# Chunk 0 of a delta-rule attention: the inverse of 64 rows kept as two blocks of 32, applied one behind the other

## The chip, the cores and the metric

The kernel runs on one core of one Trainium2 chip. Five engines work side by side, each with its own queue of instructions that it takes in order: TensorE (PE in the profile, PEld its weight loads), VectorE (DVE), ScalarE (ACT), GpSimd (POOL) and SyncE (SP), which here only issues DMA transfers. Between engines the order is kept by semaphores. The metric is the device time of one execution in microseconds (us).

## The reference

Part one is attention with a delta rule, for 4 batches, 8 heads, 768 tokens and head size 48; each head has a 48x48 state that goes from token to token. Part two takes its output, 3072 tokens with 384 features, through a layer with SiLU.

```python
k_n = k / (norm(k) + 1e-06)
for t in range(S):
    y[:, :, t] = einsum('bhd,bhde->bhe', q[:, :, t], state)
    v_old = einsum('bhde,bhd->bhe', state, k_n[:, :, t])
    state = state + beta[:, :, t] * einsum('bhd,bhe->bhde', k_n[:, :, t], v[:, :, t] - v_old)
x = y.transpose(0, 2, 1, 3).reshape(3072, 384)
h = x @ w_in                       # 384 x 2048
out = (h * (1 / (1 + exp(-h)))) @ w_out
```

The two weights arrive as 64-bit numbers and are narrowed to 32 bits on the chip; all products are in fp32, which TensorE makes in two passes.

## The kernel before

**Tiles.** The 768 tokens are six chunks of 128, a chunk is two halves of 64 tokens (0 and 1), a half two blocks of T = 32, and a block two corners of Q = 16. The 32 pairs of batch and head are taken as two groups (g = 0, 1) of 16, HH in the code. Within a half the recurrence over tokens is solved at once: with the lower triangle of the key products k k^T, scaled by beta, the new values are z = inverse x (V - what the state already holds). `score` makes the key products (pa, kept in aps[c, g][0]; those with the queries in aps[c, g][1]), `inner` applies the inverse xi to the values vf (pz, copied to zbuf), `update` adds to the states (pu), `keys` subtracts what the state holds (ph, by an addition into vf on DVE), `old` and `new` make the outputs (pyc), and for half 0 of chunk 0, where the state is zero, `first_outputs` makes them from a padded copy of z called slab (py).

**The inverse of chunk 0.** `invert_first` solves all corners of 16 at once by a loop of additions on DVE, and transposes the result twice (`low`, `up`). Corners become the inverse of 32 by `corner` (key products times `low`, scaled and completed by DVE into y), `turned` (its transpose, into xes) and `straight` (into xi). Blocks of 32 become the inverse of 64 by two `merge_half` products each. These steps, for both groups, are `joins(hf)`: half 0's run straight through, half 1's are stepped by the words j of the script. All their products are 32 rows by 32 columns, so that four lie side by side in TensorE's array.

**The layer.** A half-chunk's outputs are copied from pyc into xT (features by tokens): the odd heads go through the tile `part` and five DMA transfers by SP, the even heads straight by ACT (`even_heads`, `move`). `hidden(c, hf)` makes phid = w_in^T xT in eight pieces of 2 x 6 passes, ACT applies SiLU to gT, `project` makes po. hidden(0,0) needs half 0's outputs, hidden(0,1) half 1's.

**Narrowing.** The weights come in eight pieces each of w_in ("in", 0 to 7) and w_out ("out", 0 to 7). A piece's raw bits are loaded by SP, and then `narrow` runs two steps on ACT (L232, L233), two on DVE (L237, L241) and one on POOL (L245). f of hidden(0,0) needs piece f.

**What sets the order.** `pin` keeps each engine's instructions in program order. `in_line` does the same for SP's DMA queue and lets each transfer wait for the landing of the one two before it. So the program's order decides, and in the middle of the kernel it is written out by hand as a string of words: s is the next step of `solve`, r the next piece of hidden or project, f and b the next step or beginning of a narrowing, j steps of joins(1), T and q transposes of chunk 1's keys and queries, l its lengths, p its scores, i its inverse, w and W loads of weights. A PSUM bank (`bank`) is one of eight, taken in turn; a product into a bank waits for what last read it. From chunk 1 on nothing is changed; `merge` there does the merges.

Of the kernel before, what the change touches and what calls it, by code (L numbers as in the profile page):

```python
# [19 lines left out]
def kernel(  # L20
# [10 lines left out]
    nc = tc.nc  # L31
# [242 lines left out]
    AT_UP = AT_X + SLAB  # L274
# [63 lines left out]
    second = const.tile([P, 1], FP32, name="second")  # L338
    pin(nc.vector.tensor_reduce(out=second[:], in_=pick[:, T // 2 : T], axis=AX.X, op=ALU.add))
# [324 lines left out]
    def invert_first(step):  # L664
# [7 lines left out]
        for m in range(Q - 1, 0, -1):  # L672
# [16 lines left out]
        y = sum_room[:, AT_G : AT_G + BH * T].rearrange("p (n s) -> p n s", s=T)  # L689
        up = sum_room[:, AT_UP : AT_UP + BH * T].rearrange("p (n t) -> p n t", t=T)  # L690
        pin(nc.vector.transpose(out=low.rearrange("p n s -> p s n"), in_=x[:, 0:Q, :]))
        pin(nc.gpsimd.tensor_copy(
            out=y[:, :, Q:T], in_=pick[:, Q:T].unsqueeze(1).to_broadcast([P, BH, Q])
        ))
# [3 lines left out]
        both = work.tile([P, BH, T], FP32, name="xe_y", tag="g", bufs=1)  # L698
        xes[0], ys[0] = both[:], both[:].rearrange("p (g h) t -> p g h t", g=2)

        def heads(g, hf):
            for i in range(HH // 2):
                for e in range(2):
                    yield i, HH * g + 2 * i + e, hf ^ e ^ g

        def of_half(t, g, hf, k):
            return t[:, HH * g + (hf ^ k ^ g) : HH * (g + 1) : 2]

        def out_of(pl, to, width):
            return pl[to, 0 : HH // 2 * width].rearrange("p (n s) -> p n s", s=width)  # L710

        def corner(g, hf):

            pls = [bank(room, "pl") for room in (A, CC)]
            for i, n, k in heads(g, hf):
                for j in (2 * k, 2 * k + 1):
                    cols = slice(T * (j % 2), T * (j % 2 + 1))
                    pin(nc.tensor.matmul(
                        pls[k][rows[j], Q * i : Q * (i + 1)], lhsT=aps[0, g][0][rows[j], n % HH // H, n % H, cols],
                        rhs=low[rows[j], n, :], start=True, stop=True,  # L720
                    ))
                    yield
            for k in range(2):
                of = slice(W * k, W * (k + 1))
                pin(nc.vector.scalar_tensor_tensor(
                    out=of_half(y[of], g, hf, k)[:, :, 0:Q], in0=out_of(pls[k], of, Q), scalar=second[of],
                    in1=pick[of, 0:Q].unsqueeze(1).to_broadcast([W, HH // 2, Q]), op0=ALU.mult, op1=ALU.add,
                ))

        def turned(g, hf):  # L730

            pls = [bank(room, "pl") for room in (A, CC)]
            for i, n, k in heads(g, hf):
                pin(nc.tensor.matmul(
                    pls[k][rows[2 * k], T * i : T * (i + 1)], lhsT=up[rows[2 * k], n, :],
                    rhs=y[rows[2 * k], n, :], start=True, stop=True,
                ))
                yield
            for k, by in enumerate((by_act, by_dve)):
                by(of_half(xes[0][rows[2 * k]], g, hf, k), out_of(pls[k], rows[2 * k], T))  # L740

        def straight(g, hf):

            pls = [bank(room, "pl") for room in (A, CC)]
            for i, n, k in heads(g, hf):
                for j in (2 * k + 1, 2 * k):
                    pin(nc.tensor.matmul(
                        pls[k][rows[j], T * i : T * (i + 1)], lhsT=y[rows[j], n, :],
                        rhs=up[rows[j], n, :], start=True, stop=True,
                    ))  # L750
                    yield
            for odd in (1, 0):
                for k, by in enumerate((by_act, by_dve)):
                    j = 2 * k + odd
                    by(
                        of_half(xi[rows[j]].rearrange("p g h t -> p (g h) t"), g, hf, k)[:, :, T * odd : T * odd + T],
                        out_of(pls[k], rows[j], T),
                    )

        yield corner, turned, straight  # L760

    slab = sum_room[:, AT_X : AT_X + SLAB]
# [28 lines left out]

    def merge_half(g, hf, second):

        y = ys[0][:, g]
        pms = [bank(room, "px" if second else "py") for room in (A, CC)]
        for i in range(HH // 2):
            for e in range(2):
                n, k = 2 * i + e, hf ^ e ^ g  # L800
                even, odd = slice(W * k, W * k + T), slice(W * k + T, W * (k + 1))
                if second:
                    to, left, right = even, y[odd, n, :], xis[g][odd, n, T:W]
                else:
                    left = aps[0, g][0][even, n // H, n % H, T:W]
                    to, right = odd, xes[0][even, g * HH + n, :]
                yield pin(nc.tensor.matmul(
                    pms[k][to, T * i : T * (i + 1)], lhsT=left, rhs=right, start=True, stop=True
                ))
# [579 lines left out]

    def kept():  # L1390
        busy(1)

    def filled(n):
        return lambda: fill(n)

# [208 lines left out]
```

## Time and profile before

| | us |
|---|---|
| three runs | 642.75, 644.36 (median), 645.83 |
| the profiled execution | 643.82 |
| its span in the trace | 642.1 |
| mean granted clock of TensorE | 0.978 |
| first hidden product (phid) starts | 51.45 |
| first product of hidden(0,1) starts | 94.82 |
| first project product (po) starts | 115.62 |
| first merge of chunk 1 (py) starts | 135.37 |

A profile's line of instructions in order of time has the start, the duration, engine, line of the kernel, operation, output<-inputs, shapes and count; in brackets the idle time of the engine before it and what ended it. Lines with several instructions give the time from the first start to the last end.

### The profile page before, as it was taken

To read this page: it belongs to the slowest core of one execution; us is meant where nothing else is said; L and a number is where in the kernel's file an instruction comes from. 1 tells how busy PE (TensorE), PEld (TensorE's weight loads), DVE (VectorE), ACT (ScalarE), POOL (GpSimd) and SP (SyncE) were. 2 spreads that over 40 slices of the span, in tenths; PEclk is the share of its full clock that TensorE was granted. 3 is DMA by queue.
4 is the path that set the end of the run, shared out by engine and by line. 5 is a ranking of instruction groups with operands and counts; after the bars stand their busy time and mean duration, and the time that the engine had idled before them with its cause. 6 is when DMAs were issued, how large, how long until landed. Compare 5 with 4: busy or idle time off the path is not lost.

```text
span 642.1 us, 21892 instructions
## 1 busy us (share of the span) xinstructions
PE 621.8 (97%) x9642; PEld 546.6 (85%) x9642; DVE 404.7 (63%) x917; ACT 216.8 (34%) x512; POOL 94.8 (15%) x96
## 2 busy tenths in 40 slices
PE   6879999999999999999999999999999999999997
PEld 4778778666689989989989989989989989889997
DVE  5846879998775974755975554976565963212112
ACT  2656674152251122441122351122451122441120
POOL 5323531255020020020020020020010000000000
PEclk9759999999999999999999999999999999999999
DMA  9756354260469241469142359332163033100101
GB/s 189 168 152 195 109 125 98 74 125 3 101 128 168 43 89 21 86 122 155 39 94 31 75 121 162 57 82 31 46 140 70 22 74 41 40 13 1 26 0 26
DMA packets 141695, 53.69 MB, mean 84 GB/s; under 512 B 113296, under 2 KB 135056, under 8 KB 141600
## 3 DMA queue, kind: packets, MB, share of 16 engines
q1 hardware_dynamic: 141264, 52.14, 39.9%
q8 instruction: 76, 1.25, 0.8%
q10 hardware_dynamic: 336, 0.15, 0.1%
q14 instruction: 19, 0.16, 0.1%
HBM read 39.62 MB, written 10.49 MB: 78 GB/s over the span
## 4 chain that ended last, share of the span: by engine, by line
PE 70%; DVE 10%; DMA 8%; SPq 7%; issue 2%; ACT 1%; POOL 1%; POOLq 0%; DVEq 0%
PE phid L1044 27%; PE px L1151 13%; PE py L1151 10%; PE po L1079 7%; DVE rank L628 4%; DVE x L633 3%; PE pz L841 2%; PE pa L530 2%; SPq L197 2%; PE ph L829 2%; PE pyc L909 2%; SPq L142 1%; PE pyc L922 1%; DVE sums_of_g L1133 1%; DMA up<-x 1%
## 5 line engine op out<-in xcount | busy, mean ns | idle before, releaser
L1044 PE MATMUL phid<-xT,w_in 128*128 128x256 f32 x1152 | 258.5, 382 | 1.0 <-DMA xT<-part 0.9
L1044 PEld LDWEIGHTS phid<-xT,w_in 128*128 128x128 f32 x1152 | 215.8, 190 | 32.0 <-issue 3.0
L1054 ACT ACTIVATE gT<-phid 128x512 f32<-128x512 f32 x88 | 52.5, 598 | 142.2 <-PE phid L1044 137.6
L628 DVE SCALAR_TENSOR_TENSOR rank<-g,step,x 128x31 f32<-128x31 f32 (+15 forms) x124 | 49.7, 401 | 36.5 <-DMA g<-blocks 33.0
L1133 DVE TENSOR_TENSOR sums_of_g<-gT 128x384 f32<-128x384 f32 (+1 forms) x60 | 30.4, 525 | 57.2 <-ACT gT L1054 46.6
L1151 PE MATMUL py<-w_out,sums_of_g 128*128 128x192 f32 x320 | 56.8, 329 | 0.0
L1151 PE MATMUL px<-sums_of_w,sums_of_g 128*128 128x192 f32 x320 | 56.6, 329 | 0.0
L1151 PEld LDWEIGHTS px<-sums_of_w,sums_of_g 128*128 128x128 f32 x320 | 52.2, 190 | 0.5
L1151 PEld LDWEIGHTS py<-w_out,sums_of_g 128*128 128x128 f32 x320 | 52.2, 190 | 0.4
L633 DVE TENSOR_TENSOR x<-x,rank 128x31 f32<-128x31 f32 (+15 forms) x124 | 42.5, 342 | 4.3
L468 POOL TENSOR_TENSOR vf<-vf,n_slot 128x768 f32<-128x768 f32 x10 | 15.2, 1524 | 173.3 <-DMA vf<-in_v_dram 173.3
L868 DVE TENSOR_TENSOR state<-state,pu 48x384 f32<-48x384 f32 x44 | 24.3, 552 | 21.4 <-PE pu L861 20.4
L545 ACT COPY xT<-pyc 48x128 f32<-48x128 f32 (+2 forms) x126 | 32.6, 259 | 1.6
L489 DVE STREAM_TRANSPOSE kq<-stage 128x512 f32<-128x512 f32 x28 | 28.4, 1112 | 5.9 <-DMA stage<-in_q_dram 5.8
L1151 PE MATMUL py<-w_out,gT 128*128 128x192 f32 x160 | 28.4, 329 | 0.0
L1151 PE MATMUL px<-sums_of_w,gT 128*128 128x192 f32 x160 | 28.4, 329 | 0.0
L1151 PE MATMUL px<-w_out,gT 128*128 128x192 f32 x160 | 28.0, 327 | 0.0
L841 PEld LDWEIGHTS pz<-vf,xi 64*64 64x64 f32 x768 | 25.0, 142 | 3.2 <-issue 2.6
L551 POOL COPY g<-x 64x256 f32<-64x256 f32 x4 | 5.0, 1238 | 152.3 <-DVE x L636 152.3
L1151 PEld LDWEIGHTS px<-w_out,gT 128*128 128x128 f32 x160 | 26.4, 190 | 0.5
L841 PE MATMUL pz<-vf,xi 64*64 64x48 f32 x768 | 26.6, 226 | 0.0
L1151 PEld LDWEIGHTS py<-w_out,gT 128*128 128x128 f32 x160 | 26.1, 190 | 0.3
(197 smaller groups left out, 832.3 us busy)
## 6 DMA issues: line engine op xcount, KB each, us to landing
vf<-in_v_dram SPq DMA_DIRECT2D x48, 96.0 KB, 2.9
out_dram<-o SPq DMA_DIRECT2D x42, 96.0 KB, 2.2
w_out<-in_moe_w_in_dram SPq DMA_DIRECT2D x12, 256.0 KB, 3.3
sums_of_w<-in_moe_w_out_dram SPq DMA_DIRECT2D x8, 384.0 KB, 3.6
blocks<-ap SPq DMA_DIRECT2D x40, 64.0 KB, 1.9
g<-blocks SPq DMA_DIRECT2D x5, 512.0 KB, 3.6
kb<-in_k_dram SPq DMA_DIRECT2D x12, 192.0 KB, 4.4
kb<-in_k_dram SPq DMA_DIRECT2D x24, 96.0 KB, 4.5
```

The lines of the kernel that those rows point to most:

```text
L468: pin(nc.gpsimd.tensor_tensor(out=vf, in0=vf, in1=of, op=ALU.mult))
L489: pin(nc.vector.transpose(out=kqs[c, b][:, :, j, :].rearrange("p a (i m) -> p a m i", i=T), in_=src.rearrange("p a (m d) -> p a m d", d=D) ...
L545: return pin(nc.scalar.copy(to, of))
L628: pin(nc.vector.scalar_tensor_tensor(out=tv, in0=g[:, 0:m, m : m + 1].to_broadcast([P, m, n]), scalar=step[:, m : m + 1], in1=x[:, m : m + ...
L633: yield pin(nc.vector.tensor_tensor(out=x[:, 0:m, m:T], in0=x[:, 0:m, m:T], in1=tv, op=ALU.add))
L841: yield pin(nc.tensor.matmul(pz[rows, n * D : (n + 1) * D], lhsT=xis[g][rows, u * H + 2 * p + e, :], rhs=vfs[c][rows, hf, g * HB + u, p, : ...
L868: pin(nc.vector.tensor_tensor(out=to, in0=to, in1=by_heads(pu[of]), op=ALU.add))
L1044: pin(nc.tensor.matmul(ph[:, j * GT : (j + 1) * GT], lhsT=w_in[:, a, (2 * f + j) * P : (2 * f + j + 1) * P], rhs=xTs[c, hf][:, a, :], star ...
L1054: pin(nc.scalar.activation(out=hidden_of(c, hf, f), in_=ph[:], func=ACTF.Silu, scale=-0.5 if in_blocks(c) else 0.5))
L1079: pin(nc.tensor.matmul(pos[i][:, 0:DM], lhsT=hidden_of(0, hf, f // 2)[:, at : at + C], rhs=w_outs[f // HFF][:, f % HFF, :], start=(f == 0) ...
L1133: pin(nc.vector.tensor_tensor(out=sums_of_g[:, k, fs], in0=of[0], in1=of[1], op=op))
L1151: pin(nc.tensor.matmul(to, lhsT=at, rhs=quarter(f, *b) if isinstance(b, tuple) else sums_of_w[b][:, f], start=start and f == 0, stop=f == ...
```

## The change

Chunk 0's inverse is no longer made up to 64 rows. The blocks of 32 are kept, and applied one behind the other: `upper` multiplies the even block of 32 into the values, `cross` takes the key products between the blocks times that result and adds it to the odd block's values (an addition into vf on DVE), `lower` multiplies the odd block. `inner` for chunk 0 and the merges fall away. As the results of upper and lower share a bank by rows and columns, each bank is first set to zero by a product of the identity with zeros (`cleared`, 384 columns; once for pz, once for pw, per group and half), and the products add to it.

`corner` and `straight` become products of 64 rows: the weights are two blocks of 32 on the diagonal, with zeros beside them, so that one product serves both blocks; `turned` falls away. The corner's weights stand in xi and are copied there by POOL (`corner_scores`); its bank is preset by the identity times pick (128 columns), which takes DVE's scaling away; the result goes to a new tile `joined`, four copies by ACT (two of them by DVE for group 1, columns 64 on). After half 1's corners, xi takes the products between blocks (`cross_scores`, four copies on POOL, word C). slab moves from sum_room to the tail of `stage`.

Moved: V's loads of chunk 0 stand before the loads of chunk 1's keys; the narrowing of piece 0 begins within the loop of corner solves (word p0), so that its ACT steps stand ahead of the last score copies; V's sizing (size_half(0), POOL) and slab's clearing stand earlier; the next narrowing begins after `upper`; and the string of words is another one around chunk 0's half 1. The words behind "z" are the same.

```diff
-    AT_UP = AT_X + SLAB
+    AT_UP = AT_X + (T + 1) * T
...
-    second = const.tile([P, 1], FP32, name="second")
-    pin(nc.vector.tensor_reduce(out=second[:], in_=pick[:, T // 2 : T], axis=AX.X, op=ALU.add))
...
         def corner(g, hf):
-            pls = [bank(room, "pl") for room in (A, CC)]
-            for i, n, k in heads(g, hf):
-                for j in (2 * k, 2 * k + 1):
-                    cols = slice(T * (j % 2), T * (j % 2 + 1))
-                    pin(nc.tensor.matmul(
-                        pls[k][rows[j], Q * i : Q * (i + 1)], lhsT=aps[0, g][0][rows[j], n % HH // H, n % H, cols],
-                        rhs=low[rows[j], n, :], start=True, stop=True,
-                    ))
...
+            pc = bank((A, CC)[g], "pc")
+            yield pin(nc.tensor.matmul(
+                pc[:, 0 : HH // 2 * Q], lhsT=ident[:],
+                rhs=pick[:, 0:Q].unsqueeze(1).to_broadcast([P, HH // 2, Q]),
+                start=True, stop=False, skip_group_check=True,
+            ))
+            for i, n, of in heads(g, hf):
+                yield pin(nc.tensor.matmul(
+                    pc[of, Q * i : Q * (i + 1)], lhsT=xi[of, n // HH, n % HH, :], rhs=low[of, n, :],
+                    start=False, stop=True, skip_group_check=True,
+                ))
+            for j in range(NB):
+                at = T * (j % 2)
+                (by_dve if g == 1 and j // 2 == 1 else by_act)(
+                    joined[rows[j], g, :, at : at + Q],
+                    pc[rows[j], 0 : HH // 2 * Q].rearrange("p (i s) -> p i s", s=Q),
+                )
+        def straight(g, hf):
+            px = bank((A, CC)[g], "px")
+            for i, n, of in heads(g, hf):
+                yield pin(nc.tensor.matmul(
+                    px[of, T * i : T * (i + 1)], lhsT=joined[of, g, i, :], rhs=up[of, n, :],
+                    start=True, stop=True,
+                ))
+            of = px[:, 0 : HH // 2 * T].rearrange("p (i t) -> p i t", t=T)
+            if hf == 0:
+                (by_act, by_dve)[g](inverses[:, g], of)
+                return
+            for j in range(NB):
+                at = T * (j % 2)
+                by_act(inverse(rows[j], g, hf ^ j // 2 ^ g, at), of[rows[j]])
...
+    def cleared(room, name):
+        to = bank(room, name)
+        return to, pin(nc.tensor.matmul(
+            to[:, 0:DM], lhsT=ident[:], rhs=states[0][:, 0, 0, D:W].unsqueeze(1).to_broadcast([P, DM // (W - D), W - D]),
+            start=True, stop=False, skip_group_check=True,
+        ))
...
+    def upper(g, hf):
+        pz, done = cleared((A, CC)[g], "pz")
+        pzs[g] = pz
+        yield done
+        for u, p, e, n, _, _ in of_heads():
+            rows = blocks_of[hf ^ e ^ g][0]
+            yield pin(nc.tensor.matmul(
+                pz[rows, n * D : (n + 1) * D], lhsT=half_inverse(rows, hf, g, u * NP + p, e),
+                rhs=vfs[0][rows, hf, g * HB + u, p, :], start=False, stop=True, skip_group_check=True,
+            ))
+        (by_act, by_dve)[g](zbuf[:, g * HB : (g + 1) * HB, hf, :, 0:D], by_heads(pz))
...
     def solve(c):
         if c == 0:
-            together(inner(0, 0, 0, CC))
-            together(inner(0, 1, 0, M))
+            for step in (upper, cross, lower):
+                for g in range(2):
+                    together(step(g, 0))
+                if step == upper:
+                    begin_next()
...
-            together(inner(0, 0, 1), old(0, 0, 1))
-            yield
-            together(inner(0, 1, 1), old(0, 1, 1))
+            together(upper(0, 1), upper(1, 1))
+            yield
+            together(cross(0, 1), cross(1, 1))
+            yield
+            together(lower(0, 1), old(0, 0, 1))
+            yield
+            together(lower(1, 1), old(0, 1, 1))
...
+    load_v(0)
     load_k(1)
-    load_v(0)
...
-    begin(("in", 0))
     inv = invert_first(step)
+    joined = join_room()
+    pin(nc.gpsimd.memset(slab, 0.0))
...
-        for word in ["s2 u0 u1", "", "w0", "s3", "w1", "u2", "", "u3 w2", "", "", "", "", "w3", "", "", "", "", "", "", "", "", ""][n].split():
+        for word in ["s2 c0 u0 u1", "", "w0", "s3 c1", "w1", "u2", "", "u3 w2", "", "p0", "", "v0", "w3", "", "", "", "", "", "", "", "", ""][n].split():
...
-    together(joins(0, [none, none, none, sized, filled(2), none, filled(1), none, begin_next, none]))
+    together(joins(0, [lambda: None, filled(2), lambda: None, filled(1)]))
...
-        "s f s f T f q T s q T j5 j4 j8 j8 f j5 f q r T j20 j5 j8 j4 j16 j5 j4 b r q r f j4 j4 f W7 r b j4 f2 j4 j4 j32 r f e j6 j6 b j8 j4 f j4 j20 f j4 r j4 j99 l h f2 b l s w2 f r2 l2 p r s w3 r p r l p f l2 f l3 b l f l2 s l f l p l3 r l3 s l f l r l2 p f s2 l2 f l4 f r2 f p2 v l g r i p i p f r i r i2 r i r i b l i r f r i r b r2 i b b b i2 r2 i2 f b i5 r6 f r f r i2 r2 f r i r f r f i4 f i b r2 i3 b f b f r i r i f k r f r z i b r s r2 t z s b r2 b s m2 r5 t f t m f t m2 r s t m r b s b m r m2 s r m r m r c m2 s m r m t b m2 s m2 b m f m2 t r t m3 r m s m",
+        "s f s f T f q T s q T f b f q r T j17 b r q r f j17 f W7 r b f2 j16 r f e j99 C r f b r f r h l f2 b l s w2 f r2 l2 p r s w3 r p r l p f l2 f l3 b l f l2 p s l f l s l3 r l3 s s l f l r l2 p f s2 l2 f l4 f r2 f p2 v l g r i p i p f r i r i2 r i r i b l i r f r i r b r2 i b b b i2 r2 i2 f b i5 r6 f r f r i2 r2 f r i r f r f i4 f i b r2 i3 b f b f r i r i f k r f r z i b r s r2 t z s b r2 b s m2 r5 t f t m f t m2 r s t m r b s b m r m2 s r m r m r c m2 s m r m t b m2 s m2 b m f m2 t r t m3 r m s m",
```

141 lines of the change are left out of this document (60 added, 81 removed).

## The prediction

> **What bounds the kernel now.** First the page: busy time, the clock's row of the slices, the chain that ended last.
>
> ```profile
> PE 621.8 (97%) x9642; PEld 546.6 (85%) x9642; DVE 404.7 (63%) x917; ACT 216.8 (34%) x512; POOL 94.8 (15%) x96
> ...
> PEclk9759999999999999999999999999999999999999
> ...
> PE 70%; DVE 10%; DMA 8%; SPq 7%; issue 2%; ACT 1%; POOL 1%; POOLq 0%; DVEq 0%
> ```
>
> TensorE works 97% of the span, so a change is worth what it does to TensorE's stream. The table of stretches puts 6.1 us of its idle time behind 160 us and nearly none between 96 and 116; delay up to there isn't given back. The clock is at half only near the start. Second, the same table cut where the clock steps (columns: stretch, us, busy us of PE, its weight loads, DVE, ACT, POOL, then clock).
>
> ```profile
> 20.00:23.41 3.41, 3.41 (x40) 2.21 (x40) 3.07 (x11) 2.72 (x7) 0.00 (x0) 0.50 0.84 142
> ...
> 26.83:30.24 3.41, 2.68 (x192) 2.38 (x192) 3.35 (x5) 1.83 (x6) 3.41 (x3) 1.00 0.83 247
> 30.24:33.65 3.41, 1.75 (x49) 1.59 (x51) 1.45 (x4) 0.36 (x1) 3.08 (x3) 0.50 0.50 106
> 33.65:37.07 3.42, 2.19 (x127) 2.06 (x124) 2.12 (x5) 2.72 (x5) 1.47 (x1) 0.50 0.21 43
> ...
> 43.89:47.31 3.42, 3.42 (x81) 3.30 (x80) 1.12 (x2) 1.40 (x3) 0.00 (x0) 0.50 0.59 188
> ```
>
> A stretch that is busy throughout (20.00, 43.89) is followed by the full clock; one busy for 2.68 us (26.83) was followed by half. Third, TensorE in time order, then ACT and SP at the end of chunk 0 (start, us, and in brackets the idle time before).
>
> ```profile
> 33.42 0.69 PE L734 MATMUL pl<-sums_of_w 32*32 32x32 f32 x19 [1.47 <-issue]
> 37.15 0.91 PE L747 MATMUL pl<-sums_of_w 32*32 32x32 f32 x52 [1.31 <-issue]
> 41.81 3.54 PE L841 MATMUL pz<-vf,xi 64*64 64x48 f32 x62
> 51.45 1.46 PE L1044 MATMUL phid<-xT,w_in 128*128 128x256 f32 x6
> ...
> 86.27 1.08 PE L922 MATMUL pyc<-ap,z 64*48 64x64 f32 x64
> 87.27 2.86 PE L1044 MATMUL phid<-xT,w_in 128*128 128x256 f32 x12
> 90.06 1.16 PE L530 MATMUL pa<-stage 48*64 48x64 f32 x64
> 92.15 1.54 PE L1044 MATMUL phid<-xT,w_in 128*128 128x256 f32 x6
> 93.62 1.16 PE L530 MATMUL pa<-stage 48*64 48x64 f32 x64
> 94.82 3.48 PE L1044 MATMUL phid<-xT,w_in 128*128 128x256 f32 x15
> ```
> ```profile
> 87.41 0.58 ACT L545 COPY part<-pyc 48x512 f32<-48x512 f32 x1 [2.79 <-PE pyc L922]
> ```
> ```profile
> 90.24 3.46 SPq L902 DMA_DIRECT2D xT<-part  x5
> ```
>
> In half 0 TensorE stands 2.8 us for "issue" among the many 32-row products; these stops, and two of 0.3 and 0.2 at 29.2 and 41.0, lie 64 products (256 instructions with their weight loads) apart, and the page's instruction queue moves 1.25 MB in 76 packets, 16 KB each. From 51.45 the hidden products fill it. The last rows matter most: from the end of pyc (87.3) until hidden(0,1) starts (94.82), 7.5 us of other products cover ACT's copies and the five transfers that finish its input; its third weights, the first that need the last transfer, run 8.2 us after pyc.
>
> **The change, part by part.** I follow each engine's queue of the changed kernel, with what each instruction waits for, and put durations from rows of before on it. *Half 0.* Corner, turned, straight and merges were 224 products; now corner and straight are 64. ACT narrows piece 0 before its last score copies (28.97 + 1.8 = 30.8), copies six corner groups at 0.25 (32.3), DVE two at 0.29. Straight runs from 31.8, 64 passes at 0.054 (the pz row above, half clock), to 35.2. Nothing stops TensorE between 33.65 and 37.07, so I take the full clock from 37.07. Then come four clears (384 columns, two passes of 0.327 as in po: 0.65 each, 1.3 at half) and six groups of 32 passes at 0.027 (0.87): upper, cross and lower end at 44.0; two first_outputs at 0.87 and six turns at 0.5 make it 48.8 at the first hidden product, for 51.45. Bounds: 46.2 at full clock from 30.24, 50.5 at half until 47.31. More than 0.3 us of an earlier start would be lost again, because ACT comes to piece 5 at 57.8 and its raw weights landed at 57.5.
>
> *TensorE's work from 48.8 to the first project product.* 192 hidden passes at 0.2175 (41.8), turns 1.0, two presets 0.44, corner and straight 1.74 each, pu twice 1.74, ph 1.1, chunk 1's scores 256 passes at 0.018 (4.6), four clears 2.6, upper and cross 0.8 each, lower with old 2.0, new 0.87, pg 0.4: 61.6, so 110.4 without a wait; before it was 115.7. That is -5.3.
>
> *The waits in it.* (1) ACT's queue from 47.8: five turn copies 2.5, pieces 2 to 5 7.2, two gT 1.0, six corner copies 1.5: 60.0. DVE's last two corner copies wait for it (60.6) and hold DVE's queue, with piece 4 behind them; straight, reached at 59.4, waits 1.25. (2) DVE narrows piece 4 (0.69 + 0.96) to 62.3; POOL merges it (1.85), sizes V (1.47), squares K (1.8) to 67.4; DVE sums lengths (0.5), adds four state parts (2.27) and does piece 5 (0.96): 71.2; POOL's 1.85 gives 73.0. Hidden f5, reached at 69.6, waits 3.4. (3) Piece 6 stands behind keys' two vf additions on DVE: ph's end + 1.02 + 1.65 + 1.85 = 4.5, while f5's rest and 32 passes of scores cover 1.9. f6 waits 2.6. (4) ACT's narrowing of out0 and out1 now stands ahead of the score copies whose bank cross's clear takes; out1's transfers are issued behind four blocks transfers, and land 7.5 us after those start (78.0 + 7.5 = 85.5). Two narrowing steps 1.8, two copies 0.7 and z's copy 0.5 let cross start at 88.5 for 85.75: 2.75. DVE's added vf additions (0.55 each) and z copies cost lower 0.4. (5) Between new and hidden(0,1) only f7's second part (1.3) and two of its own weights (0.9) are left; the third comes 8.2 after new, as before: 6.0. Score products that covered it now come behind it.
>
> Together 16.5 with 0.1 at the state add. So 16.5 - 5.3 = +11.2. A bound for each wait is nothing below; above, (1) and (2) grow by 2.6 with half clock in half 0, (5) by the 0.5 to 1.5 us that the out3 transfers now ahead of it may add (landing medians 3.4 for its own, 5.2 for theirs).
>
> *The clock after wait (5).* It empties most of the stretch 101.9 to 105.3 (busy 1.0 of 3.41). Rows: 1.45 busy at 9.76 was followed by half clock, as was 2.68 at 26.83, but 2.44 at 173.60 by full. I take one stretch at half, 1.7 us, between nothing and 5 (the shorter waits halve stretches too). Sum +12.9: 643.82 + 12.9 = 656.7. That execution lies 0.5 under the median of 644.36, within the runs' 642.75 to 645.83.
>
> The Trainium skill (TensorE: Matmul & The Clock Gate, Part 1: The HAM clock gate) lets the clock fall only after about 3.4 us without work; the row at 26.83, with 0.73 us idle, disagrees. By that rule alone wait (5) would be the only one to slow the clock, and the sum is 656.7; by that row waits (2) to (4) slow it too, and it is 660.
>
> *Costed at nothing.* V before K(1): V is wanted at 36.5, and K(1), landing at about 29.4 in its place, at the turns at 44.9; were it late, the turns would wait one for one. POOL's room, corner copies and cleared slab lie in 12.7 us of its idle time before 25.96, cross_scores' four copies (0.78 each) in its 5.2 us before piece 2 and 3.0 before piece 3, since piece 4 reaches POOL only at 62.3. SP: out3's two issues pass xT's five; the second waits for the gather of blocks, 88.0 + 2.2 + 3.5 + 3.6 = 97.3, and xT's data is ready at 99.0; if that cover of 1.7 goes, hidden(0,1) is later by as much. Chunk 1's inverse starts 13.7 us later, but its merge too, behind 34 project products for 30.
>
> **The rivals.** *Likeliest, 0.55:* the waits as found, 656.7, its own range 650 to 660. *The clock falls at the shorter waits too, 0.14:* ph ends 2.4 later, cross another 0.9, and with (5) that is 660 to 663. For it the row at 26.83, against it the one at 173.60. *The blocks of products are again short of instructions, 0.06:* the 2.8 us of "issue" stay, and the waits move with ACT's queue: 659.5; against it, 64 products of 64 rows take 3.4 us at full clock, more with their clears, where 64 of 32 rows took 1.5 at 0.012 a pass. *Narrowing is in time, only wait (5) stays, 0.14:* ACT is only 59% busy between 54 and 60, so pieces 4 to 6 could come sooner than the queue says: 643.8 - 5.3 + 6.0 = 644.5, or 646.2 and more with clock and small waits. *Faster, 0.11:* TensorE's own work decides, as its 97% suggests; place: 48.8 to the first project product; price 5.3, hence 638.5 with every wait covered. It decides for faster while the waits sum to under 2.1, and for not slower under 5.3; against it, wait (5) alone has rows for 6.0.
>
> **The numbers.** A change of 0.5%, 3.2 us, is about what a measurement can tell. Faster 0.11; same 0.10 (the fourth case without its 0.04 beyond 647); slower 0.79. Range 645 to 663: it leaves out the faster case and half of the fourth, and takes in the ends of the clock.
>
> **What would show it.** First hidden product between 46 and 50.5, no idle "issue" over 0.5 us before; idle TensorE before f5 (by POOL's merge), before f6, before cross (by ACT) and 5 to 7 us before the third product of hidden(0,1) (by xT's transfers); the first project product near 127, half clock in at least one stretch near 105. I am wrong if that product comes before 119, or if TensorE's idle time between 50 and 128 is under 8 us.

## The result and the profile after

The changed kernel takes 698.74 us (median of four runs, 697.19 to 700.97), the kernel before 645.1 in the same comparison (642.75 to 645.83). The ratio is 1.0841, 95% interval 1.0798 to 1.0884. The profiled execution took 699.24, with a span of 697.5 for 642.1 before. Slower was forecast, but as 656.7 (645 to 663): the loss is over four times the forecast one.

From the page of the changed kernel: busy times, and the row of the granted clock in 40 slices of 17.4 us.

```profile
PE 667.8 (96%) x9282; PEld 574.7 (82%) x9282; DVE 397.7 (57%) x900; ACT 216.2 (31%) x514; POOL 102.1 (15%) x112
...
PEclk8659876689999999999999999999999999999999
```

TensorE has 360 passes fewer than before and is busy 46 us longer. So most of the loss is not idle time: the same kinds of products take longer. The clock's row, which was below 9 in two slices only, is now below 9 in eight of the first nine, up to 157 us.

To see where the loss arises, compare the starts of the same product, counted from the beginning, in the two traces: the first hidden product comes 5.4 us later (56.81 for 51.45), the 97th hidden pass (the first of hidden(0,1)) 40.0 later, the first project product 48.4 later (164.04 for 115.62), the end 55.4 later. Four fifths of it lie between the first hidden product and the first project product. The table cuts this stretch by kinds of products. Each entry is the time from the start of one product to the start of the next, put down to the first of the two and summed, so a wait counts with the product ahead of it.

| us between the first hidden and the first project product | before | after |
|---|---|---|
| hidden (192 passes) | 43.9 | 57.2 |
| scores of chunk 1 (256) | 6.5 | 11.6 |
| corners, straight, merges of half 1 (before 388, after 132) | 6.9 | 5.4 |
| inner or upper, cross, lower, with clears; old and new | 3.0 | 27.6 |
| states, keys, lengths, turns | 3.9 | 5.4 |
| all | 64.2 | 107.2 |

The fourth row alone holds 24.6 us of the 43. TensorE in order of time shows why (start, us from first start to last end, engine, line, operation, count). First the kernel before, where `inner` (L841) and `old` (L909) go in turn; then the changed kernel, where L876 is `lower` and L941 is `old`.

```profile
79.90 0.21 PE L841 MATMUL pz<-vf,xi 64*64 64x48 f32 x2
79.92 0.22 PE L909 MATMUL pyc<-kq,state 48*48 48x64 f32 x2
79.95 0.22 PE L841 MATMUL pz<-vf,xi 64*64 64x48 f32 x2
```

```profile
101.84 1.55 PE L864 MATMUL pw<-z,xi 32*32 32x48 f32 x64
103.32 1.56 PE L1083 MATMUL phid<-xT,w_in 128*128 128x256 f32 x6
104.81 0.27 PE L876 MATMUL pz<-vf,xi 32*32 32x48 f32 x2
105.01 0.31 PE L941 MATMUL pyc<-kq,state 48*48 48x64 f32 x2
105.25 0.27 PE L876 MATMUL pz<-vf,xi 32*32 32x48 f32 x2
...
123.66 0.36 PE L876 MATMUL pz<-vf,xi 32*32 32x48 f32 x2
123.95 0.45 PE L941 MATMUL pyc<-kq,state 48*48 48x64 f32 x2
```

Before, a product of two passes starts about every 0.03 us, though two kinds are in turn. In the changed kernel 64 passes of cross, all of one size, take 1.55 us. The 128 passes of lower and old, issued in turn (`together` takes one product of each), take from 104.81 to 124.33: 19.5 us, one product every 0.22 us and from 108.3 on every 0.33. The durations of the single instructions hardly differ: at full clock a pass takes 213 ns (lower) and 235 (old) in these turns, 219 and 217 in the turns of the kernel before. No line shows idle time, as the groups with shapes kept apart tell (busy us, mean ns of one over both clocks, idle; the first holds the `old` of later chunks too):

```profile
L941 PE MATMUL pyc<-kq,state 48*48 48x64 f32 x576 | 29.2, 227 | 0.0
L876 PE MATMUL pz<-vf,xi 32*32 32x48 f32 x64 | 10.8, 262 | 0.0
```

One product lasts about as long as ever; what is lost is most of their overlap. The second thing to read is the clock. The table of stretches, cut where the clock steps (stretch, us, busy us of PE with its passes, granted clock, DMA share, GB/s):

```profile
33.30:53.70 20.40, 20.40 (x315) 0.50 0.52 143
53.80:81.00 27.20, 24.52 (x364) 1.00 0.48 157
81.10:94.60 13.50, 11.79 (x122) 0.50 0.14 21
94.60:108.30 13.70, 12.52 (x238) 1.00 0.43 111
108.40:128.80 20.40, 20.40 (x178) 0.50 0.12 42
```

Half clock for 20.4 us although the trace shows TensorE never idle, twice: once with half 0's 64-row and 32-row products and the four clears among them, once in and behind the turns of lower and old. The half clock from 81.1 to 94.6 follows a wait. The idle times of TensorE that answer to the forecast's five waits (idle time and its releaser in brackets):

```profile
69.41 1.11 PE L722 MATMUL px<-sums_of_w,joined 64*64 64x32 f32 x30 [0.33 <-DVE joined L546]
81.98 2.93 PE L1083 MATMUL phid<-xT,w_in 128*128 128x256 f32 x6 [3.09 <-POOL w_in L245]
91.55 2.93 PE L1083 MATMUL phid<-xT,w_in 128*128 128x256 f32 x6 [0.83 <-POOL w_in L245]
101.00 0.91 PE L771 MATMUL pw<-state,ident 128*128 128x384 f32 x2 [0.75 <-ACT ap L543]
134.85 0.67 PE L1083 MATMUL phid<-xT,w_in 128*128 128x256 f32 x2 [3.63 <-DMA xT<-part]
```

All five are there, each by the releaser that it named; the last stands mostly before the first product of hidden(0,1), not before the third. The 0.4 us forecast ahead of lower isn't there.

### The profile page after: what moved, and what is told of

It is laid out like the page before. It is cut to its first block, busy times and chain, and to the rows that moved or that the text cites. A ratio compares the mean times of both kernels' runs of the same rounds, so it can differ in the third digit from the quotient of the medians.

```text
span 697.5 us, 21179 instructions
## 1 busy us (share of the span) xinstructions
PE 667.8 (96%) x9282; PEld 574.7 (82%) x9282; DVE 397.7 (57%) x900; ACT 216.2 (31%) x514; POOL 102.1 (15%) x112
## 4 chain that ended last, share of the span: by engine, by line
PE 66%; DVE 13%; DMA 10%; SPq 4%; issue 2%; ACT 2%; POOL 1%; POOLq 0%; DVEq 0%; ACTq 0%
PE phid L1083 23%; PE px L1190 10%; PE py L1190 8%; PE po L1118 6%; DVE rank L626 5%; DVE x L631 5%; PE pa L528 3%; PE pyc L941 3%; DMA up<-x 2%; DVE sums_of_g L1172 2%; PE ph L820 2%; DMA xe<-low 2%; PE pz L832 2%; PE pyc L954 2%; DMA g<-blocks 2%
## 5 line engine op out<-in xcount | busy, mean ns | idle before, releaser
L1083 PE MATMUL phid<-xT,w_in 128*128 128x256 f32 x1152 | 267.1, 390 | 8.7 <-DMA xT<-part 4.2
L1083 PEld LDWEIGHTS phid<-xT,w_in 128*128 128x128 f32 x1152 | 220.4, 194 | 42.2 <-POOL w_in L245 4.2
L900 DVE TENSOR_TENSOR state<-state,pu 48x384 f32<-48x384 f32 x44 | 24.3, 552 | 25.6 <-PE pu L893 24.7
L1190 PE MATMUL px<-w_out,gT 128*128 128x192 f32 x160 | 29.7, 341 | 0.0
L941 PE MATMUL pyc<-kq,state 48*48 48x64 f32 x576 | 29.2, 227 | 0.0
L1190 PEld LDWEIGHTS px<-w_out,gT 128*128 128x128 f32 x160 | 28.0, 199 | 0.5
L538 DVE TENSOR_TENSOR ap<-pa,above 128x256 f32<-128x256 f32 x40 | 14.8, 419 | 20.4 <-PE pa L528 10.0
```

The costliest lines, as they stand in the source:

```text
L900: pin(nc.vector.tensor_tensor(out=to, in0=to, in1=by_heads(pu[of]), op=ALU.add))
L941: yield pin(nc.tensor.matmul(py[to, C * p + W * u : C * p + W * (u + 1)], lhsT=states[g][of, u, p, 0:D], rhs=kqs[c, g * HB + u][of, p, 1, ...
L1083: pin(nc.tensor.matmul(ph[:, j * GT : (j + 1) * GT], lhsT=w_in[:, a, (2 * f + j) * P : (2 * f + j + 1) * P], rhs=xTs[c, hf][:, a, :], star ...
L1190: pin(nc.tensor.matmul(to, lhsT=at, rhs=quarter(f, *b) if isinstance(b, tuple) else sums_of_w[b][:, f], start=start and f == 0, stop=f == ...
```

## The experiments

**Turns of two sizes (1): the same products, sorted.** The theory: a change of the tile's size from one product to the next costs TensorE its overlap. The rival: the 32-row products, or the loads of half 1, are slow of themselves.

```diff
-            together(lower(0, 1), old(0, 0, 1))
+            together(lower(0, 1), lower(1, 1))
             yield
-            together(lower(1, 1), old(0, 1, 1))
+            together(old(0, 0, 1), old(0, 1, 1))
```

> The changed kernel with lower and old of half 1 issued one after the other instead of product by product in turn. Theory (turns between tiles of 32 rows and of 64 rows cost TensorE a drain each): the 19.5 us that the two took from 104.8 to 124.3 become under 4, the half clock from 108.4 to 128.9 goes or shortens, and the time falls by 17 to 21 us to 678-682. Rival (lower itself is slow, because its results share a bank with upper's): lower alone takes over 8 us, and the time falls by less than 8.

Measured: 678.42 us (677.08 to 681.59), ratio to before 1.0478 (1.0404 to 1.0552), 20.3 under the changed kernel. In the trace:

```profile
104.51 1.55 PE L876 MATMUL pz<-vf,xi 32*32 32x48 f32 x64
105.99 0.31 PE L941 MATMUL pyc<-kq,state 48*48 48x64 f32 x2
106.68 1.99 PE L941 MATMUL pyc<-kq,state 48*48 48x64 f32 x62 [0.38 <-ACT z L543]
```

The same 128 passes take 4.1 us instead of 19.5, and the half clock from 108 to 129 is gone. The order of these products, not their number, cost 20 us: two fifths of the whole loss.

**Turns of two sizes (2): the cost by itself.** Behind the kernel before, patterns of products on loaded weights, with 128-row products between them.

```diff
+    for i in range(32):
+        small(b32[i % 2], b32[i % 2], t1)
+        small(o48[i % 2], HALVES[1 - i % 2], t2)
+    warm()
+    for i in range(32):
+        small(b32[i % 2], b32[i % 2], t1)
+    for i in range(32):
+        small(o48[i % 2], HALVES[1 - i % 2], t2)
...
+        small(HALVES[i % 2], HALVES[i % 2], t1)
+        small(o48[i % 2], HALVES[1 - i % 2], t2)
...
+        small(HALVES[i % 2], HALVES[i % 2], t1)
+        small(whole, whole, t2)
...
+    for i in range(100):
+        small(b32[i % 2], b32[i % 2], (t1, t2)[i % 2], 2 * P)
```

> The kernel before, with products appended behind its last store whose results nobody reads; its own work is unchanged and the appended patterns are read from the trace, each after 48 full-size passes. Theory: 32 pairs of a 32-row tile and a 48-row tile in turn take 12 to 15 us at full clock (0.2 us a turn); the same 64 products sorted by size take under 3; 64-row and 48-row tiles in turn under 3, as in the kernel before; 64-row tiles and full-size products in turn also pay at each turn. Rival (the loss needs the kernel's data or banks): 32-row and 48-row in turn under 4 us. Last pattern: 200 passes of 32-row tiles with 256 columns without a gap; if the clock follows the wall-busy time of the trace it stays full, if it follows how much of the array works it falls to half within two stretches of 3.4 us.

One run, 793.79 us. Stretches within the patterns (same columns): 32 and 48 rows in turn at full and at half clock; 32 rows alone; 48 alone; 64 and 48 in turn; 32 rows alone with 256 columns.

```profile
651.00:654.00 3.00, 3.00 (x29) 1.00 0.00 0
655.00:671.00 16.00, 16.00 (x94) 0.50 0.00 1
683.00:684.30 1.30, 1.30 (x64) 1.00 0.00 0
684.50:686.00 1.50, 1.50 (x54) 1.00 0.00 0
697.00:698.50 1.50, 1.50 (x105) 1.00 0.00 0
749.00:769.00 20.00, 20.00 (x188) 1.00 0.00 1
```

From start to start, a pass takes 0.110 us in turn (0.167 at half clock), 0.021 and 0.029 sorted; the sorted pair takes 3.5 us in all, a little over the 3 expected. 64 and 48 rows in turn take 0.015, so these two count as one size here; 64 and 128 rows in turn take 0.148 (0.242). In both slow patterns the clock fell to half, 3.4 us into the first and 6.0 into the second, without idle time in the trace. The first pattern takes 19.6 us: that is the changed kernel's 104.81 to 124.33 again, without the kernel. The weight loads show where the gap lies: in turn, the load for the next size starts only 0.13 to 0.15 us after the start of the last pass before it, and its product 0.002 us behind the load; sorted, loads start 0.01 to 0.04 us apart while products run. What holds the load back is not shown. The last pattern kept the full clock, which by the expectation speaks for the trace's busy time as what the clock follows; the second set of patterns, below, takes that up from half clock.

**Turns of two sizes (3): the same in the kernel before.** There `inner` of half 1 and `old` also go in turn, with 64-row tiles. Here inner's products use one 32-row block; three quarters of its work are left out.

```diff
+        small = (c, hf) == (0, 1)
...
+            if small:
+                rows = slice(rows.start + T, rows.stop)
             yield pin(nc.tensor.matmul(
-                pz[rows, n * D : (n + 1) * D], lhsT=xis[g][rows, u * H + 2 * p + e, :],
+                pz[rows, n * D : (n + 1) * D], lhsT=xis[g][rows, u * H + 2 * p + e, T if small else 0 : W],
```

> The kernel before with one thing changed: inner of half 1 of chunk 0, which runs in turn with old, multiplies the last 32 of 64 rows alone (three quarters of that product are left out, so its output is not the reference's). Theory (tile sizes in turn): 64 products of inner and 64 of old, 2.2 us before, take 14 to 20, and the kernel is 12 to 20 us slower than before though it does less. Rival (the new products in some other way): no change, within 2 us.

One run, 664.84 us for 645.62: +19.2, with less work. In the trace (the last line is a group with its shape):

```profile
82.01 0.27 PE L844 MATMUL pz<-vf,xi 32*32 32x48 f32 x2
82.21 0.31 PE L916 MATMUL pyc<-kq,state 48*48 48x64 f32 x2
82.45 0.27 PE L844 MATMUL pz<-vf,xi 32*32 32x48 f32 x2
...
L844 PE MATMUL pz<-vf,xi 32*32 32x48 f32 x64 | 9.8, 240 | 0.0
```

The same 0.44 us for a pair as in the changed kernel. So the turns are enough for such a loss, whatever else the change did.

**Which difference of size counts.** Are common rows needed, or is it the width; does it help to group?

```diff
+    for i in range(32):
+        small(r3, r3, t1)            # rows 96 to 127, 32 columns
+        small(o0, h0, t2)            # rows 0 to 47, columns 0 to 63
...
+        small(r3, r3, t1)
+        small(r3, HI, t2)            # rows 96 to 127, 64 columns
...
+        small((r3, o0)[i // 4 % 2], (r3, h0)[i // 4 % 2], (t1, t2)[i // 4 % 2])
...
+    for i in range(100):
+        small((r1, r3)[i % 2], (r1, r3)[i % 2], (t1, t2)[i % 2], 2 * P)
+    for i in range(60):
+        small(HALVES[i % 2], HALVES[i % 2], (t1, t2)[i % 2], 2 * P)
```

> The kernel before with more products appended whose results nobody reads. Theory (a turn drains TensorE whenever the tile's height changes): 32 rows in turn with 48 rows cost 0.2 us a turn even where the two share no rows and columns of the array; 32 rows to 32 columns in turn with 32 rows to 64 columns cost little; groups of four pay once a group, so a quarter. Rival (only tiles that overlap drain): the first pattern takes under 4 us. For the clock, the last two patterns start from half clock: 32-row tiles of 256 columns back to back for 20 us, then 64-row tiles. If how much of the array works counts, the clock stays at half through the first and comes back in the second or with the full-size products; if only uninterrupted streaming counts, it comes back within 7 us of the first.

One run, 822.84 us. Stretches: the first pattern at full clock; groups of four; then, from a half clock, the 200 passes of 32-row products without a gap (they end at 783.7) with the first eight 64-row passes, the next 3.4 us of 64-row products, and those after.

```profile
651.50:654.00 2.50, 2.50 (x25) 1.00 0.00 0
715.80:719.80 4.00, 4.00 (x64) 1.00 0.00 0
741.00:785.30 44.30, 44.30 (x208) 0.50 0.00 1
785.40:788.80 3.40, 3.40 (x18) 0.51 0.00 0
788.90:800.00 11.10, 11.10 (x101) 1.00 0.01 1
```

Tiles that share neither rows nor columns pay the same 0.110 us a pass. Tiles of the same 32 rows that differ in width alone pay 0.109: the expectation that this costs little was wrong. Groups of four take 0.065: fewer turns cost less, but not in proportion. The last three lines belong to the clock and are read below.

**The clears.** `upper` and `cross` write their two blocks' rows by themselves and each row block is copied or added alone, so no bank has to be zero.

```diff
-        pz, done = cleared((A, CC)[g], "pz")
-        pzs[g] = pz
-        yield done
+        pz = pzs[g] = bank((A, CC)[g], "pz")
...
-        (by_act, by_dve)[g](zbuf[:, g * HB : (g + 1) * HB, hf, :, 0:D], by_heads(pz))
+        for rows, _ in blocks_of:
+            (by_act, by_dve)[g](zbuf[rows, g * HB : (g + 1) * HB, hf, :, 0:D], by_heads(pz[rows]))
...
-        pw, done = cleared((A, CC)[g], "pw")
-        yield done
+        pw = bank((A, CC)[g], "pw")
```

> The changed kernel without the eight clears; the results of upper and cross are taken out by two groups of 32 rows each instead of all 128. The clears took 6.6 us in half 0 (at half clock) and 3.2 in half 1. Theory (half 0 is TensorE work in a row): the first hidden product comes 5 to 6.5 us earlier and the time falls by 5 to 9. Rival (the clears, being full-size, are what brings the clock back): the half clock lasts longer and half of that is lost.

One run, 688.71 us, 10.0 under the changed kernel. The first hidden product starts at 51.49, 5.3 sooner; four clears of 1.65 us at half clock stood ahead of it. From there to the first project product only 0.5 us more is gained, although half 1's four clears went too: cross now waits 3.8 us and hidden f6 2.6. The other 4.7 us in the trace lie behind the first project product, where nothing was edited: chunk merges wait 0.9 us for transfers of `low` instead of 4.0, and a stretch of 3.4 us at half clock (292.7 to 296.1) is missing.

**Both together.** The edits of the first and the clears experiment.

> The changed kernel with both edits: lower and old apart, and no clears. Apart alone gave -20.3 us, no clears alone -10.0. Theory (two separate costs): 666 to 670. Rival (the clears' gain in half 1 hid in the slow interleaving): 671 to 676.

Measured: 676.99 us (674.69 to 680.82), ratio 1.0504 (1.0453 to 1.0556): no better than sorting alone (678.42), so the expected sum missed. The first hidden product is 4.6 us sooner than with sorting alone, the first project product only 2.0, and these lines (TensorE in order of time) tell where the rest went:

```profile
94.36 2.77 PE L854 MATMUL pw<-z,xi 32*32 32x48 f32 x64 [3.61 <-ACT z L543]
...
116.06 2.41 PE L1074 MATMUL phid<-xT,w_in 128*128 128x256 f32 x4 [3.63 <-DMA xT<-part]
```

Cross, ahead of which TensorE idles 0.9 us with sorting alone, waits 3.6 us here, at half clock; the clears had stood where TensorE now waits. There ACT's and POOL's queues set the time, and TensorE arrives sooner only to wait.

**Is it the clock, or the wait itself?** The last kernel with six full-size products before f5 and seven before hidden(0,1), into a bank that is written over, so that these waits are not idle.

```diff
+            for _ in range({(0, 0, 5): 6, (0, 1, 0): 7}.get((c, hf, f), 0)):
+                pin(nc.tensor.matmul(
+                    ph[:, 0:GT], lhsT=w_in[:, 0, 0:P], rhs=xTs[0, 0][:, 0, :], start=True, stop=True,
+                ))
```

> The kernel with both edits, and work added where TensorE waits: 6 full-size products (12 passes, 2.6 us at full clock) ahead of hidden f5 and 7 ahead of the first product of hidden(0,1), into the bank that the hidden product then overwrites; nothing is left out. Theory (a long wait costs more than its length, because half clock follows it): the half clock after both waits goes or shortens, and the time falls by 4 to 9 us although work is added. Rival (only the wait's length costs): no change within 2, or longer by up to 5.

Measured: 675.12 us (671.58 to 677.43), ratio 1.0465 (1.0413 to 1.0517), 1.9 under the last. The half clock behind f5 moved from 77.7 to 84.7 us, behind f6's wait. The one near 91 to 108 stayed, and the one behind xT only became shorter (118.8 to 125.5 for 115.3 to 125.4). So this neither shows nor excludes the clock as the price of these two waits. Filling a wait did not keep the clock at full here.

**Cover for xT.** From the kernel without turns and clears: a piece of hidden(0,0) that stood ahead of the last products of half 1 is moved behind them, between the outputs and hidden(0,1).

```diff
-… l3 s s l f l r l2 p f s2 l2 f l4 f r2 f p2 v l g r i …
+… l3 s s l f l l2 p f s2 l2 f l4 f r2 f p2 v l g r2 i …
```

> The kernel with both edits, and two words moved in the string: hidden f7's first part and the two parts of hidden(0,1)'s first piece come later, so that f7 (2.6 us), two score groups and the length products stand between new and hidden(0,1). Theory (wait 5 of the prediction: xT's transfers are ready 8 us after new): the wait of 3.6 us on xT's transfers falls under 1, the half clock after it goes, and the time falls by 5 to 9. Rival (the wait moves to another place, pa or lower): less than 2.

Measured: 669.92 us (665.87 to 674.76), ratio 1.0392 (1.032 to 1.0464): 7.1 less. TensorE's wait for xT falls from 3.9 us to 1.8 in four parts of at most 0.8, and the half clock behind it is gone. More than the wait went; the half clock behind it went too. The four runs spread over 9 us, so the 7.1 is rough; in the two traces the first project product comes 9.1 sooner.

**Narrowing sooner.** From there: f's steps are moved forward, and one b that starts another piece is taken out, so that pieces 5 and 6 reach POOL sooner.

```diff
-… C r f b r f r h l f2 b l s w2 f r2 l2 p r s w3 … l3 b l f l2 p …
+… C r f b r f r h l f3 b l s w2 f r2 l2 p r f2 s w3 … l3 l f l2 p …
```

> The kernel with lower and old apart, no clears and xT covered, and the words of the string moved once more: piece 5's last narrowing step ahead of the lengths and state additions, piece 6's steps ahead of keys, and out1's narrowing behind the score copies and upper's copies. Theory (waits 2, 3 and 4 of the prediction, each with the half clock that follows): the waits of 3.1 (f5), 2.6 (f6) and 3.8 (cross) go, the half clock from 77.5 to 81 and 91 to 101 goes or shortens, and the time falls by 10 to 16 us to 654-660. Rival (they come back at other instructions): above 666.

Measured: 659.3 us (656.48 to 661.78), ratio 1.0218 (1.0183 to 1.0252): 10.6 less. TensorE's remaining waits are these:

```profile
79.36 1.56 PE L1074 MATMUL phid<-xT,w_in 128*128 128x256 f32 x6 [0.59 <-POOL w_in L245]
...
85.42 1.55 PE L854 MATMUL pw<-z,xi 32*32 32x48 f32 x64 [1.17 <-ACT z L543]
...
102.09 0.67 PE L1074 MATMUL phid<-xT,w_in 128*128 128x256 f32 x2 [0.59 <-DMA xT<-part]
```

The wait before f5 (3.09 in the kernel that it starts from) is gone, f6's is 0.6 for 2.6, cross's 1.2 for 3.8, and of the half clock between the first hidden and the first project product one stretch of 3.4 us is left (87.3 to 90.7). The idle time that went is 7.8 us of the 10.6; the half clock that went (77.5 to 80.8 and most of 91.2 to 101.3) accounts for more than the rest. In the two traces the first project product comes 10.7 us sooner, the end 7.0: the rest is lost again in the chunks behind.

**The clears again, without the waits.**

> The same order of work as the run beside it, with the eight clears back. Theory (with the waits gone the clears only cost their own time: 5.3 us in half 0, 2.6 in half 1): 6 to 9 us above the run beside it. Rival (the clears pay for themselves by the clock, as in the kernels with waits): within 3 of it.

The last kernel with its clears back: 669.67 us (667.4 to 673.32), ratio 1.0399 (1.0363 to 1.0435), 10.4 over it. That is more than the 6 to 9 expected; in the two traces it is 8.5, with 5.4 ahead of the first hidden product, 2.1 from there to the first project product and 1.0 behind it. So the clears cost about their own time where no wait behind them takes it in. Where one does, they cost little: in the single removal half 1's brought 0.5 us, and with both together the 4.6 us of half 0's shrank to 2.0.

**The moves alone.** The kernel before, with V's loads ahead of the keys', the narrowing of piece 0 within the loop of corner solves, and V's sizing there.

```diff
-    load_k(1)
     load_v(0)
+    load_k(1)
...
-    begin(("in", 0))
...
-… "u3 w2", "", "", "", "", "w3", …
+… "u3 w2", "", "p0", "", "v0", "w3", …
```

> The kernel before with only the moved parts of the change: V loaded ahead of chunk 1's keys, piece 0 narrowed from within the loop of corner solves, V sized there too. Theory (these are covered): within 1.5 us of before. Rival (SP's order or ACT's two steps ahead of the score copies cost something): slower by 2 to 5.

Measured over ten runs: 646.23 us (642.12 to 647.02), ratio 1.0007 (0.9981 to 1.0032). These moves cost and bring nothing that can be told (within 0.3%).

**POOL's copies beside DVE's lengths.** In the changed kernel DVE's small instructions ahead of the corner solves are slower. DVE in order of time, first of the changed kernel, then of the last experiment, where POOL has no tile `joined` to fill:

```profile
15.09 1.23 DVE L421 SCALAR_TENSOR_TENSOR spread<-nr,nt 32x32 f32<-32x32 f32 x4
```
```profile
14.34 0.77 DVE L423 SCALAR_TENSOR_TENSOR spread<-nr,nt 32x32 f32<-32x32 f32 x4
```

Four of DVE's instructions beside POOL's work on `joined` are longer than in the other kernel. They end at 14.16, 15.05, 15.48 and 15.92, each 0.03 to 0.04 us after a POOL instruction ends (14.13, 15.01, 15.44, 15.88). The reciprocal among them (0.35 us) and the transpose behind them (1.25) take the same in both.

The kernel with the sooner narrowing, with `joined`'s filling and slab's clearing written later in the program, and the first copy of corner_scores one step later too:

```diff
-    joined = join_room()
-    pin(nc.gpsimd.memset(slab, 0.0))
...
+        if n == 1:
+            joined = join_room()
+            pin(nc.gpsimd.memset(slab, 0.0))
```

> The best of the changed order so far (lower and old apart, no clears, xT covered, narrowing sooner), and POOL fills the tile joined and clears slab after DVE's first lengths instead of beside them. In the changed kernel's trace DVE's last steps of the lengths took 1.0 us longer than before, beside POOL's copies. Theory (the two engines get in each other's way): the lengths end 1 us earlier, the corner's first product comes 1 us earlier, and the time falls by 0.5 to 2. Rival (the copies then slow the loop of corner solves as much): no change.

Measured: 658.12 us (656.85 to 666.03), ratio 1.0243 (1.0166 to 1.0319), no change against 659.3 that can be told. But the edit did not move POOL's work on `joined`: POOL clears `joined` at 13.19 and copies at 14.20, in the changed kernel at 13.18 and 14.19, since nothing on POOL stands between and POOL waits for no place of DVE. What a later filling would give is therefore open. No experiment came out faster than the kernel before.

## Why the prediction was wrong, step by step

**"Lower with old 2.0" is the step that failed.** It measured 19.5 us (104.81 to 124.33). The price was taken from rows of before in which inner and old go in turn at 0.016 us a pass. There both are of one size by the patterns' measure (64 and 48 rows: 0.015 a pass); with 32 rows in place of 64 the same turns cost 0.110. The nearest row differed in the one thing that counted, and neither bounds nor rivals held it. Even with 2.0 in place of the 19.5 the kernel would have come out above the range, as the 678.42 of the sorted kernel shows: the steps below failed too. Of the 19.5 us, 128 passes at 0.110 are 14.1; the other 5.4 are the half clock, which came 3.5 us into the turns. The three experiments on turns show the step: minus 20.3 without them, plus 19.2 with them in the kernel before, and the price by itself.

**First hidden product, 48.8 with bounds 46.2 to 50.5: seen at 56.81.** The first straight products start 0.9 later than counted, with DVE's lengths a microsecond slower, and straight ends 1.6 later than counted. The bulk is the clock: I took it as full from 37.07, since nothing idles there; it stayed at half to 53.7 with TensorE busy throughout. The reading behind it, that a stretch that is busy throughout is followed by the full clock, held for the two rows of before (20.00, 43.89) and failed here. Clears, upper, cross and lower then took 14.3 us (36.82 to 51.08) for 8.8, outputs and turns 5.7 for 4.8. Even the upper bound ended the half clock at 47.3, as in before. What held: the stops for "issue" are gone (at most 0.3 us idle in that stretch).

**The waits.** (1) 1.25 forecast, 0.57 seen; (2) 3.4, seen 3.09; (3) 2.6, seen 0.83; (4) 2.75 ahead of cross, seen 0.75, with 0.43 at the scores ahead of it that the forecast didn't have, and 0.4 ahead of lower, not seen; (5) 6.0, seen 4.43 (3.63, 0.55 and 0.25). The main releasers are right. Waits (3) and (4) are short here, with half clock from 81.1 to 94.6 and the clears ahead of them; in the kernel without clears they are 2.6 and 3.8, and the narrowing and xT experiments take most of them, and of (5), away at minus 10.6 and minus 7.1.

**The clock after wait (5), 1.7.** Measured at half: 81.1 to 94.6 behind wait (2), 135.7 to 145.8 behind wait (5). The rival that the clock falls at the shorter waits too, given 0.14, was right in its mechanism, though not in its time. Up to the first project product the clock was at half for 78.5 us in the changed kernel, for 27.3 before: 51.2 more, where the forecast had one stretch of 3.4. At half speed that is up to 25.6 us of the loss, an estimate from these two numbers, which overlaps with the turns' 5.4 and with what half 0 lost ahead of the first hidden product. The rule that I weighed, of the Trainium skill (TensorE: Matmul & The Clock Gate, Part 1: The HAM clock gate), has the clock fall after a window of about 3.4 us without work; here it fell at 108.3 and in the patterns of unlike sizes in turn, with no idle time in the trace. The measurement decides: by it, the row at 26.83 was the better guide, though no rule either: in the changed kernel a stretch as empty (98.1 to 101.5, 2.66 us busy) was followed by the full clock.

**Costed at nothing.** The moves of V, piece 0 and V's sizing: right, 1.0007. POOL's room in idle time: not quite, DVE's lengths end 1.0 us later with it.

**My own signs of error.** The first project product was to come near 127, and came at 164. TensorE's idle time between 50 and 128 was to be over 8 us, and is 5.7 (0.24, 0.33, 3.09, 0.83, 0.43, 0.75). By that sign the waits were not the main cause, and they were not. But wait (5) had moved out of that stretch: up to the first project product TensorE idles 10.1, for 16.5 forecast.

**The sum of the 53.6 us** goes along the chain of experiments, by medians, so each term is uncertain by some 5 us: turns 20.3; clears 1.4 at that place, 10.4 where no wait hides them; cover for xT 7.1; narrowing and the waits behind it 10.6; and 14.1 remain in the kernel with 659.3. The delay of the first project product in the traces falls along the same chain with less scatter: 17.5, 2.0, 9.1, 10.7, and 9.1 remain. Of the 14.1 (15.1 in its profiled execution) its trace puts 9.1 before the first project product: chunk 0's upper, cross, lower, old and new at 9.7 for 3.0, hidden at 47.4 for 43.9, corners and straight at 5.4 for 6.9, the rest nearly equal. The other 6.0 come later, the largest part (2.7) around chunk 2's merge; in them are 2.2 us more of waits for transfers of `low`, and 3.4 us at half clock (251.1 to 254.5). In all the changed kernels this later part, which no edit touches, takes 528.7 to 533.5 us for 526.5. In the changed kernel these merges wait 4.0 us in all for transfers of `low`, for 0.2 before; the loop on DVE ahead of chunk 2's merge starts 49.9 us later than before, at the landing of the gather of blocks in both, TensorE's stream there 49.3. What made DVE later than TensorE by that, and whether that alone makes the waits, was not tried and stays open.

## What to carry to other kernels

Before a price is taken from a row, compare the sizes of the tiles on both sides of it, and above all which product stands next to which: where two chains of small products are issued in turn, give them one tile size or sort them. A wait and a stretch of small products can also cost clock behind them, so cost them with the clock that they leave, not with the clock that they find. Taking work off an engine that is about to wait gave little here until the wait was taken away (1.4 us with the waits, 10.4 without).

## What the runs showed of the hardware

- Successive products of different tile size lose most of their overlap: 0.110 us a pass at full and 0.167 at half clock for 32 rows in turn with 48, against 0.021 and 0.029 sorted, also with no common rows or columns (0.110), and for 32 against 64 columns alone (0.109). 64 rows in turn with 48 don't (0.015). Products of different banks and inputs but of one size do overlap: in half 0 the starts of the last cross and the first lower products mix within 0.3 us (48.38 to 48.63). The Trainium skill (TensorE: Matmul & The Clock Gate, Part 3: Packing small matmuls — row/col tiling) has products in different parts of the array overlap; the sorted rows agree, the rows in turn of two sizes do not.
- The clock depends on how much of the array works, not on the trace's idle time alone. From half clock, 42.8 us of gapless 32-row products left it at half, and it rose 5.1 us into the 64-row products behind them. From full clock, the same 32-row products held it full for 21.7 us, and turns of two sizes let it fall 2.7 to 6.0 us after they began. So what holds it and what raises it differ.
- Beside POOL's filling and copies of `joined`, DVE's small instructions took longer (four of 32x32 1.23 us for 0.77) and ended 0.03 to 0.04 us behind POOL's; no run tried the two engines by themselves.
